# Register loads of the expert counts, with and without the sequencer's range check

## The chip, the cores and the metric

The kernel runs as one program on one core of a Trainium2 chip. The metric is the device time of one execution in microseconds (us), lower is better. The core has five engines that run beside each other and meet only at semaphores: TensorE (PE in the profile, its weight loads PEld), VectorE (DVE), ScalarE (ACT), GpSimd (POOL) and SyncE (SP, which issues most DMAs). Each engine takes its instructions strictly from its own queue. A small processor at the head of each queue, the sequencer (PEq, PEldq, SPq and so on in the profile), handles waits, register loads and register arithmetic itself.

## The reference

Causal attention with a data-dependent bias, then a dense layer pair with a gated activation, then a mixture of eight experts with one expert per token. The change touches the last part alone.

```python
logits = x @ w_gate                      # x: 1152 x 512, 8 experts
expert_idx = np.argmax(logits, axis=1)
...
for i in range(N):                       # each token takes the next place of its expert
    e = expert_idx[i]
    if counts[e] < capacity:
        disp[e, counts[e]] = x[i]
        counts[e] += 1
...
h = np.maximum(np.einsum('ecd,edf->ecf', disp, w1), 0.0)   # w1: 8 x 512 x 1024
y = np.einsum('ecf,efd->ecd', h, w2)                       # w2: 8 x 1024 x 512
out[i] = gate_w[i] * y[expert_idx[i], pos[i]]              # for the tokens that were kept
```

How many tokens an expert gets is known only on the chip.

## The kernel before

A planner (`pl.op`) takes every operation with its engine, what it reads and writes and a rank, and fixes at build time the order in which each engine's queue holds them. Nothing is reordered on the chip.

The expert stage starts near 334 us. The experts are sorted by their token counts, the fullest first, and run as experts e = 0 to 7 of this order with fixed tile widths WR = 224, 200, 184, 168, 152, 144, 136, 128. For each expert:

- `w_unit` loads the weights in 512 KB pieces through a ring of buffers (`wraw`, issued by SP at L1448 and L1450). ScalarE makes the rounded high part of each piece (L1455), VectorE the low part by a subtraction (L1456).
- `xs_in` loads the expert's rows (SP, L1518), TensorE transposes them (L1530), and ScalarE and VectorE split them again (L1534, L1536, L1539). A small VectorE copy (L1543) takes the gate and the token number out of the loaded rows.
- `e_mm1(e, fc)`, eight times: four matmuls with the high weights (L1568), which cover the high and the low activations side by side, so twice the tile width, and four with the low weights (L1572). ScalarE copies the right half out (L1582), VectorE adds (L1584), and L1586, L1588 and L1591 make the high, low and bf16 forms of the hidden values.
- `e_mm2(e, dc)`, four times: eight matmuls of each kind (L1605 high, L1607 low), then L1612 (ScalarE) and L1614 (VectorE) add the halves, and TensorE transposes the result back (L1619).
- the result is scaled by the gate and scattered to the output by a GpSimd DMA (L1641).

TensorE's queue interleaves `e_mm2` of expert e with `e_mm1` of expert e+1. Two PSUM banks serve `e_mm1` in turn (MI and MX in the profile).

The matmuls with low weights run over as many columns as the expert has tokens, not over the full width. The counts stand in `cntI` (8 integers in SBUF). The last two VectorE operations that make them cut them off above at the tile width and below at WMIN = 64. `widths()` brings them to TensorE: its sequencer loads the eight integers into registers (L1461) and sets eight shape registers from them, four at a time (L1463). The matmuls of experts 1 to 7 then take their width from these. Those of expert 0 have fixed widths. The planner puts `widths()` behind the last `e_mm1` of expert 0 and a group of transposes, and ahead of the first `e_mm2` of expert 0.

The profile names a buffer by the first tile that held its memory. So in the expert stage xT, gtH and their bf16 neighbours xTb, gtB hold activations and hidden values, wvi holds the sums of `e_mm1`, x2R rows, and x2Tt the result of `e_mm2`. AV, MI, MX and SC are PSUM banks.

Of the kernel before, what the change touches and what calls it, by code (L numbers as in the profile page):

```python
# [388 lines left out]
def fused_kernel(ctx, tc, q, k, v, s, w_in, w_out, w_gate, w1, w2, cap, out):  # L389
    nc = tc.nc  # L390
# [3 lines left out]
    E = w_gate.shape[1]  # L394
# [7 lines left out]
    W = 256  # L402
# [593 lines left out]
    with tc.manual_schedule():  # L996
# [89 lines left out]
        cntI = bp.tile([P, E], I32, name="cntI")  # L1086
        WMIN = 64
# [370 lines left out]

        def widths():
            def ld():  # L1460
                cs = nc.values_load_multi_w_load_instructions(cntI[0:1, 0:E], engines=[mybir.EngineType.PE], min_val=WMIN, max_val=W)[1]  # L1461
                for n in range(0, E, 4):
                    nc.tensor.move_shape(wreg[n:n + 4], [[(1, c)] for c in cs[n:n + 4]])  # L1463
            pl.op("pe", 600, ld, r=["cntI", ("hT", 0, 4)], w=["wreg"])
# [359 lines left out]
```

## Time and profile before

| | us |
|---|---|
| median of 3 runs | 491.97 |
| lowest and highest of them | 488.69, 493.15 |
| the profiled execution | 487.6 |
| its span, first to last instruction | 485.9 |
| busy in it: TensorE | 456.7 (94%) |
| busy in it: VectorE, ScalarE, GpSimd | 362.3, 332.5, 124.3 |

The rows come from the one profiled execution. Times in them are microseconds from the start of its span. Busy time doesn't count register loads, checks, branches or waits, which the sequencer handles. A bracket at the end of a row gives the idle time of the engine ahead of it and what ended it; "issue" means that no semaphore that the profile shows ended it. PEclk is the granted share of TensorE's 2.4 GHz clock (0.50 is 1.2 GHz).

### The profile page before, as it was taken

The numbers are of one execution on the slowest core, as the hardware profiler recorded it, in microseconds if no ns is written. First come the engines' busy times: TensorE is split into PE (matmuls) and PEld (weight loads), VectorE is DVE, ScalarE is ACT, GpSimd is POOL, SyncE is SP. The second block draws the span as 40 slices with busy tenths as digits, with TensorE's granted clock in tenths as the row PEclk, the third lists the DMA queues.
The fourth block names the chain that finished last, engine by engine and source line by source line (L and its number), as shares of the span: only waits on it lengthen the run. The fifth ranks groups of instructions, "written<-read, shape, count | busy, mean of one in ns | idle before, by whom it ended". The sixth has DMA issues, their size and how long they took to land.

```text
span 485.9 us, 9859 instructions
## 1 busy us (share of the span) xinstructions
PE 456.7 (94%) x3458; PEld 348.4 (72%) x3460; DVE 362.3 (75%) x826; ACT 332.5 (68%) x785; POOL 124.3 (26%) x136
## 2 busy tenths in 40 slices
PE   6698889999999999999999999999869999999993
PEld 5375566667777666668767867759768888889882
DVE  7889668988989999953123466937957979999891
ACT  3878879886657766744245246834958889989981
POOL 5627567477122222210000040002000201111141
PEclk9889989999999999999999999999989999999998
DMA  8999998699954554980000159841784867888811
GB/s 162 267 237 204 219 200 171 161 198 181 218 201 161 155 190 138 355 238 1 1 0 1 58 204 348 260 122 45 208 320 113 249 216 252 276 292 255 278 63 41
DMA packets 99049, 88.22 MB, mean 182 GB/s; under 512 B 66679, under 2 KB 77943, under 8 KB 98982
## 3 DMA queue, kind: packets, MB, share of 16 engines
q1 hardware_dynamic: 97108, 82.04, 62.4%
q0 software_dynamic: 1888, 5.52, 3.0%
q8 instruction: 28, 0.46, 0.4%
q14 instruction: 25, 0.20, 0.1%
HBM read 60.60 MB, written 14.19 MB: 154 GB/s over the span
## 4 chain that ended last, share of the span: by engine, by line
PE 72%; DMA 8%; ACT 8%; issue 4%; POOL 4%; DVE 2%; SPq 0%; POOLq 0%; ACTq 0%; DVEq 0%
PE SC L610 11%; PE MI L577 8%; PE MX L577 6%; PE AV L1605 6%; PE SC L611 5%; PE SC L863 4%; DMA PT<-ph 4%; PE MI L581 4%; PE MI L1568 3%; PE MX L1568 3%; PE AV L610 3%; PE MX L581 3%; POOL ph L908 2%; PE AV L941 2%; PE AV L1607 2%
## 5 line engine op out<-in xcount | busy, mean ns | idle before, releaser
L610 PE MATMUL SC<-woH,gtH 128*128 128x512 f32 x212 | 76.6, 479 | 0.0
L863 PE MATMUL SC<-QK 128*128 128x512 f32 (+4 forms) x192 | 63.0, 434 | 6.4 <-ACT pexp L894 3.4
L908 POOL TENSOR_TENSOR ph<-pexp,ph 128x512 f16<-128x512 f32 (+4 forms) x32 | 45.3, 1415 | 31.0 <-DVE ph L848 19.1
L591 DVE SCALAR_TENSOR_TENSOR gtH<-th,gtH 128x384 fp32r<-128x384 f32 x46 | 26.1, 569 | 32.8 <-ACT gtH L589 32.3
L577 PE MATMUL MI<-xT,wiH 128*128 128x384 f32 x216 | 47.1, 357 | 0.0
L894 ACT ACTIVATE pexp<-SC,smA 64x64 f32<-64x64 f32 (+4 forms) x80 | 38.3, 521 | 12.5 <-DVE smA L885 10.7
L594 ACT ACTIVATE gtB<-th 128x384 bf16<-128x384 f32 x46 | 23.8, 519 | 32.3 <-PE SC L611 26.1
L610 PEld LDWEIGHTS SC<-woH,gtH 128*128 128x128 f32 x212 | 40.0, 194 | 3.3
L863 PEld LDWEIGHTS SC<-QK 128*128 128x128 f32 (+1 forms) x192 | 28.3, 188 | 18.8 <-issue 11.2
L1456 DVE TENSOR_TENSOR wiL<-wraw,wiH 128x1024 bf16<-128x1024 f32 x32 | 38.8, 1219 | 3.5 <-ACT wiH L1455 3.5
L611 PE MATMUL SC<-woL,gtB 128*128 128x512 bf16 x106 | 41.4, 390 | 0.0
L1456 DVE TENSOR_TENSOR woL<-wraw,woH 128x1024 bf16<-128x1024 f32 x32 | 39.0, 1218 | 2.9 <-ACT woH L1455 2.8
L611 PEld LDWEIGHTS <-gtB 128*128 128x128 bf16 x138 | 13.3, 96 | 37.5 <-issue 37.5
L1271 POOL DMA_INDIRECT xs_d<-x2R,small x9 | 9.0, 998 | 121.0 <-ACT x2Tt L1204 69.0
L553 POOL TENSOR_TENSOR wiL<-wvi,wiH 128x512 bf16<-128x512 f32 x16 | 22.5, 1404 | 65.2 <-ACT wiH L549 65.2
L1641 POOL DMA_INDIRECT out_dram<-x2R,small x8 | 9.1, 1140 | 117.1 <-ACT x2R L1668 68.7
L577 PEld LDWEIGHTS MI<-xT,wiH 128*128 128x128 f32 x216 | 37.9, 189 | 1.3 <-DVE th L587 0.3
L577 PE MATMUL MX<-xT,wiH 128*128 128x384 f32 x168 | 36.7, 359 | 0.0
L1455 ACT ACTIVATE woH<-wraw 128x1024 fp32r<-128x1024 f32 x32 | 34.1, 1065 | 1.1 <-DMA wraw<-in_moe_w_dram 1.1
L1455 ACT ACTIVATE wiH<-wraw 128x1024 fp32r<-128x1024 f32 x32 | 33.6, 1055 | 1.6 <-DMA wraw<-in_moe_w_dram 1.6
L577 PEld LDWEIGHTS MX<-xT,wiH 128*128 128x128 f32 x168 | 30.0, 189 | 0.8
L941 PE MATMUL AV<-V,PT 128*128 128x65 f16 (+1 forms) x640 | 25.8, 197 | 4.6 <-DMA PT<-ph 4.6
(280 smaller groups left out, 1148.8 us busy)
## 6 DMA issues: line engine op xcount, KB each, us to landing
wraw<-in_moe_w_dram SPq DMA_DIRECT2D x64, 512.0 KB
wraw<-in_moe_w_in_dram SPq DMA_DIRECT2D x16, 512.0 KB
wraw<-in_moe_w_out_dram SPq DMA_DIRECT2D x16, 512.0 KB
xs_d<-x2R SPq DMA_DIRECT2D x16, 257.0 KB
kraw<-in_k_dram SPq DMA_DIRECT2D x8, 288.0 KB
qraw<-in_q_dram SPq DMA_DIRECT2D x8, 288.0 KB
out_dram<-x2R SPq DMA_DIRECT2D x9, 256.0 KB
x2R<-xs_d SPq DMA_DIRECT2D x8, 257.0 KB
```

The source lines that it names most:

```text
L577: nc.tensor.matmul(ps, lhsT=whi[:, kc], rhs=xT[:, a, kc, cs], start=(kc == 0 and a == 0), stop=False)
L581: nc.tensor.matmul(ps, lhsT=wlo[:, kc], rhs=xTb[:, kc, cs], start=False, stop=(kc == KC - 1))
L610: nc.tensor.matmul(o, lhsT=gh[:, a, ts], rhs=whi, start=(fc == 0 and a == 0), stop=False)
L611: nc.tensor.matmul(o, lhsT=gb[:, ts], rhs=wlo, start=False, stop=(fc == NFC - 1))
L863: nc.tensor.matmul(o[:rows, j0:j1], lhsT=t_[:, 2 * r, i0:i0 + rows], rhs=t_[:, 2 * r + 1, j0:j1], start=True, stop=False)
L894: pl.op("act", t_act(wdt, False, 1), lambda o=o, r=r, nm=nm: nc.scalar.activation(out=pe[:rows, r, :wdt], in_=o[:rows, :wdt], func=AF.Exp, ...
L908: pl.op(eng, (t_pool if eng == "pool" else t_dve)(n * T_), lambda rs_=rs_, e_=e_: e_.tensor_tensor(out=hl[:, rs_, 0:T_], in0=pe[:rows, rs_ ...
L941: nc.tensor.matmul(av[:, slot, r, 0:D + 1 - h_], lhsT=PT[t][:, r * (1 + 2 * t) + pb, :], rhs=rhs, start=(i == 0), stop=(i == len(m) - 1))
L1455: pl.op("act", t_act(1024), lambda: nc.scalar.activation(out=dhi, in_=raw, func=AF.Copy), r=[rk], w=kh, rank=rank, after=after)
L1456: pl.op("dve", t_dve(1024), lambda: nc.vector.tensor_tensor(out=dlo, in0=raw, in1=dhi.bitcast(F32), op=ALU.subtract), r=[rk, ks[0], ks[2]] ...
L1568: nc.tensor.matmul(ps[:, 0:2 * w_], lhsT=uH[s_][kc][:, fs], rhs=xs[:, kc], start=(kc == 0), stop=False)
L1605: nc.tensor.matmul(ps[:, 0:2 * w_], lhsT=uH[s_][KC + fc // 2][:, ds_[fc]], rhs=h[:, fc], start=(fc == 0), stop=False)
```

## The change

The register load is told not to check the values' range on the chip. The minimum and maximum stay as what the build may assume of the values.

```diff
         def widths():
             def ld():
-                cs = nc.values_load_multi_w_load_instructions(cntI[0:1, 0:E], engines=[mybir.EngineType.PE], min_val=WMIN, max_val=W)[1]
+                cs = nc.values_load_multi_w_load_instructions(cntI[0:1, 0:E], engines=[mybir.EngineType.PE], min_val=WMIN, max_val=W,
+                                                                   skip_runtime_bounds_check_because="the counts are bounded on VectorE")[1]
                 for n in range(0, E, 4):
                     nc.tensor.move_shape(wreg[n:n + 4], [[(1, c)] for c in cs[n:n + 4]])
```

The added source line moves every later line number up by one. On TensorE's queue, behind the transposes of an expert's rows (SC from x2R) and ahead of the first `e_mm2` of expert 0 (AV), there stood the load of the counts, sixteen sequencer instructions, which are eight pairs of a register operation and an assertion, and the two settings of four shape registers each.

```order
L1530 MATMUL SC_105<-identF,x2R 128x128 x2
L1530 MATMUL SC_105<-identF,x2R 128x72 x2
L1461 TENSOR_LOAD cntI
L1461 ISA x16
L1463 ISA x2
L1605 MATMUL AV_107<-xT,wiH_1939 128x448 x2
```

Now the same place on the same queue has the load and the two settings alone.

```order
L1531 MATMUL SC_105<-identF,x2R 128x128 x2
L1531 MATMUL SC_105<-identF,x2R 128x72 x2
L1461 TENSOR_LOAD cntI
L1464 ISA x2
L1606 MATMUL AV_107<-xT,wiH_1939 128x448 x2
```

The sixteen are gone. No other instruction of this queue and none of the other four has moved, and no wait is added or taken away.

## Rows read from the trace of the kernel before

**Rows 1.** Lines 1461 and 1463: count, ns shortest/median/longest, first and last start.

```profile
L1461 PEldq FUSED_REGOPS  x8: 146/146/160, 353.6 to 355.7; - x8
L1461 PEldq SEQ_ASSERT  x8: 18/18/28, 353.8 to 355.9; - x8
...
L1461 PEldq TENSOR_LOAD <-cntI x1: 780/780/780, 352.7 to 352.7; - x1
...
L1463 PEldq MOVE  x2: 29/31/33, 355.9 to 356.2; - x2
L1463 PEld MOVE_SHAPE  x2: 113/116/118, 356.0 to 356.3; - x2
```

**Rows 2.** TensorE timeline, 351 to 358 us: start, us, engine.

```profile
352.23 0.52 PE L1530 MATMUL SC<-identF,x2R 128*128 128x128 f32 x4
356.46 1.83 PE L1605 MATMUL AV<-xT,wiH 128*128 128x448 f32 x4 [3.72 <-issue]
```

**Rows 3.** Windows of 1 us, with their column names.

```profile
core 0: us, PE busy (x) PEld busy (x) DVE busy (x) ACT busy (x) POOL busy (x), PEclk, DMA share, GB/s
...
355.00:356.00 1.00, 0.00 (x0) 0.00 (x0) 0.00 (x0) 0.41 (x2) 0.00 (x0) 0.94 1.03 320
...
359.00:360.00 1.00, 1.00 (x9) 0.72 (x8) 0.19 (x1) 0.00 (x0) 0.00 (x0) 0.86 0.86 311
```

**Rows 4.** Chain that ended last, from 356 us: start, us, what.

```profile
356.46 3.15 PE AV L1605 x8
...
360.40 0.74 PE MI L1568 x4
...
362.48 0.22 PE SC L1619 x2
362.70 0.74 PE MI L1568 x4
...
365.25 1.81 PE AV L1605 x8
367.06 0.78 PE AV L1607 x8
```

**Rows 5.** ScalarE and VectorE timeline around the wait: start, us, engine.

```profile
353.47 0.29 DVE L1588 SCALAR_TENSOR_TENSOR xT<-wvi,xT 128x128 fp32r<-128x128 f32 x1
...
356.62 0.16 DVE L1543 COPY small<-x2R 56x2 f32<-56x2 f32 x1 [1.91 <-DMA x2R<-xs_d]
...
357.98 1.21 DVE L1456 TENSOR_TENSOR wiL<-wraw,wiH 128x1024 bf16<-128x1024 f32 x1
360.83 0.39 DVE L1614 TENSOR_TENSOR x2Tt<-AV,x2R 128x224 f32<-128x224 f32 x1 [1.64 <-ACT x2R L1612]
361.89 0.37 DVE L1584 TENSOR_TENSOR wvi<-MI,wvi 128x200 f32<-128x200 f32 x1 [0.67 <-ACT wvi L1582]
```

**Rows 6.** TensorE timeline, 352 us to the end: its later waits.

```profile
434.32 0.44 PE L1530 MATMUL SC<-identF,x2R 128*128 128x128 f32 x2 [0.46 <-ACT gtB L1539]
...
460.97 0.44 PE L1619 MATMUL SC<-identF,x2Tt 128*128 128x128 f32 x2 [0.48 <-DVE x2Tt L1614]
```

**Rows 7.** Timeline of ScalarE, 368 to 436 us.

```profile
377.75 0.36 ACT L1612 ACTIVATE x2R<-AV 128x224 f32<-128x224 f32 x1 [1.11 <-PE AV L1607]
...
414.46 0.30 ACT L1582 ACTIVATE wvi<-MI 128x152 f32<-128x152 f32 x1 [0.38 <-PE MI L1572]
```

**Rows 8.** Timeline of all engines, 470 us to the end.

```profile
478.20 0.69 ACT L1653 ACTIVATE x2R<-SC,small 128x512 f32<-128x512 f32 x1 [1.64 <-PE SC L1634]
```

**Rows 9.** Timeline of TensorE, 60 to 70 us.

```profile
66.09 1.71 PE L941 MATMUL AV<-V,PT 128*128 128x65 f16 x28 [1.36 <-DMA PT<-ph]
```

**Rows 10.** Windows around earlier waits of TensorE, columns as above.

```profile
66.10:69.10 3.00, 3.00 (x35) 2.83 (x36) 1.24 (x4) 0.94 (x4) 0.30 (x1) 0.50 1.29 188
...
105.40:106.60 1.20, 0.11 (x5) 0.08 (x3) 0.47 (x2) 1.15 (x4) 0.22 (x1) 1.00 1.05 234
...
21.40:28.10 6.70, 5.11 (x43) 4.19 (x44) 5.63 (x7) 4.33 (x10) 3.08 (x2) 0.50 1.21 198
```

## The prediction

> **What bounds the kernel now.** I first looked for where the removed instructions ran, in the source view of their line [rows 1]. The load of the counts takes 0.78 us from 352.7. Behind it come eight pairs, a FUSED_REGOPS of 146 ns and a SEQ_ASSERT of 18 ns, from 353.6 on; the first setting of shape registers begins only at 355.9. Next I read what TensorE did meanwhile [rows 2]: its transposes end at 352.75 (352.23 plus 0.52), the next matmul starts at 356.46, and the 3.72 us between are put down to "issue", that is, to no semaphore. So the wait is the sequencer's own work, and the reader sees in it the load, the checks and the settings, end to end.
>
> Third, the granted clock [rows 3]. It fell to half within the window from 355, whose mean is 0.94: a share of (1 - 0.94)/0.5 = 0.12 us at half speed, so it fell at 355.88, after TensorE had done nothing for 3.1 us. The window from 359 gives 0.86, so 0.28 us at half speed, and the clock rose at 359.28, after 2.8 us of dense matmuls. The two `e_mm2` groups of equal shape show the price [rows 4]: the first takes 360.40 - 356.46 = 3.94 us, the second 1.81 + 0.78 = 2.59. The wait therefore cost a further 1.35 us behind itself.
>
> Fourth, is TensorE the bound behind 356? Its timeline shows only two waits of it on another engine from there to the end, 0.46 us at 434.32 and 0.48 at 460.97 [rows 6]. ScalarE on its side waited for TensorE, 1.11 us at 377.75 and still 0.38 us at 414.46 [rows 7], and its last scaling at 478.20 waited for TensorE's last matmul [rows 8]. A lead won at 356 should thus travel to the end, unless something beside TensorE holds the start of the stage.
>
> **The change part by part.** *The checks.* Sixteen instructions go, and nothing takes their place. Their price is the time from the first of them to the first setting, 355.9 - 353.6 = 2.3 us, or 0.29 us a pair; the pairs' own 164 ns would give 1.3 us, but the gaps between sequencer instructions go with them. Nothing covers them, since TensorE's queue is in order and idle. The load's 0.78 us and the settings' 0.5 us stay. The first `e_mm2` then starts at 356.46 - 2.3 = 354.16. Its inputs are there: the last hidden value of expert 0 is made at 353.47 + 0.29 = 353.76 [rows 5]. If the register values were late behind the load, the settings would wait; the row before shows the first check 0.1 us behind the load's end, so I put this at 0 to 0.1 us and take 0.
>
> *The clock.* TensorE's idle time shrinks to 3.72 - 2.3 = 1.4 us. I look for waits of that length [rows 9, 10]. One of 1.09 us, in the window from 105.4, kept the full clock (1.00, with 0.11 us busy out of 1.2). One of 1.36 us ahead of 66.09, in a stretch of 64-column matmuls, was followed by half speed (0.50 from 66.1 to 69.1). Here matmuls of 256 columns stand ahead of the wait and of 448 behind it, which is far denser work than at 66, so I take it that the clock stays; the other case is a rival.
>
> The Trainium skill, page "TensorE: Matmul & The Clock Gate", section "HAM oscillation — how this bites in real kernels", prices time at the half clock at half its length. For 355.88 to 359.28 this is an estimate of 1.7 us against 1.35 by the rows, where TensorE still stood idle for the first 0.58 us of it. The removed wait would be worth 4.0 us by the page and 3.65 by the rows; the next step cuts either to the same sum.
>
> *What is late next.* With the full clock the first `e_mm2` ends at 354.16 + 2.59 = 356.75. The two `e_mm1` groups of expert 1 behind it took 362.48 - 360.40 = 2.08 us [rows 4], so TensorE reaches the transposes L1619 at 358.83. These need VectorE's sum L1614, and here the rows of VectorE decide [rows 5]. Its copy L1543 waited 1.91 us for a DMA and began at 356.62; two weight subtractions stand behind it, the second from 357.98 to 359.19, and only then L1614. (ScalarE's copy L1612, which L1614 also needs, is no later: L1614 began 0.43 us behind the matmuls' end at 360.40, which would be 357.2.) In the old trace VectorE then idled 1.64 us for TensorE. Now TensorE waits for it: nothing of this VectorE work depends on TensorE's wait, so it stays where it is. L1614 runs from 359.19 to 359.58, L1584 (0.37 us) to 359.95. The third `e_mm1` of expert 1 needs that addition, because it writes the bank that L1584 empties. It starts at 359.96 instead of 362.70, 2.7 us earlier. So of 3.65 us won at the first matmul 0.9 is given back within 5 us.
>
> *Behind it.* VectorE's own queue moves by 361.89 - 359.58 = 2.3 us, and ScalarE, the conversions and the loads that they release follow it. TensorE had 0.4 us to spare on that addition (ended 362.26, used at 362.70), so 2.3 to 2.7 us reach the dense stretch; I take 2.7, because ScalarE's idle 1.11 us at 377.75 absorbs the difference. No instruction elsewhere changes, and the tail behind 478 keeps its length.
>
> The sum: -2.3 (checks) - 1.35 (clock) + 0.9 (VectorE) = -2.7 us. The profiled execution would go from 487.6 to 484.9. The median shown is 491.97, 4.4 above that execution, and I carry the difference over: 489.3 us, 0.5% less. About 1% is what a measurement of this kernel can tell from no change; its three runs alone lie 0.9% apart.
>
> **The rivals.** *The clock falls all the same.* For it speaks the wait of 1.36 us at 66, against it the one of 1.09 at 105 and the denser work here. Taking one stretch as long as 355.88 to 359.28 (3.4 us), TensorE loses 1.7 us, the point 358.83 becomes 360.53, VectorE no longer holds anything, and the third `e_mm1` starts near 360.75: 2.0 us won, 490.0 us. The Trainium skill, page "TensorE: Matmul & The Clock Gate", section "What's actually happening", calls the throttled state the default that activity lifts; by it two short waits could bring the fall that one long one brought here.
>
> *The lead is lost at 434.* There TensorE waited 0.46 us for ScalarE [rows 6], behind weight conversions. If those ran at the pace of their loads and not of TensorE, TensorE would come 2.7 us earlier and wait 2.7 us longer, and 0 to 0.5 us would remain: 491.5 to 492.0. Against it: ScalarE waited for TensorE at 414.46 [rows 7], so its run up to 434 was released by TensorE and moves with it.
>
> *VectorE doesn't hold.* If the load behind its copy at 356.62 lands earlier in most executions, all 3.65 us stay: 488.3.
>
> *The checks cost nothing of their own*, because the registers' arrival sets the pace: then the settings start no earlier, and the time stays 492.0. Against it, the pairs run in equal steps to the end with no long first one.
>
> *Slower.* The clock falls at the first short wait and, since a second wait of 0.8 us follows at 358.8, isn't given back for long. At 21.4 to 28.1 it stayed at half for 6.7 us although TensorE was busy for 5.1 of them [rows 10]. A stretch of that length costs about 3.4 us of matmul time against the 3.65 won, so it is no loss yet. From a little over 7 us on the kernel is slower; three stretches like the 3.4 us one (10.2 us) would cost 5.1 and give 493.4. Against it, the dense matmuls behind the wait lifted the clock within 2.8 us in this very place.
>
> **How the numbers follow.** Forecast 489.3: 0.60. Clock falls all the same, 490.0: 0.15. Lead lost at 434, 491.5 to 492.0: 0.12. VectorE doesn't hold, 488.3: 0.06. Checks cost nothing, 492.0: 0.04. Slower, 493.4: 0.03. A median of three runs that spread over 4.5 us moves by an estimated third of that, 1.5. The range goes from 488.3 less 1.8 to 490.0 plus 1.9, so 486.5 to 491.9, and leaves out about the three upper rivals. A gain of over 1% (below 487.05) needs the forecast or the 488.3 and a lucky scatter of two or three us: 0.13. A loss of over 1% needs more than the slower rival's 493.4: 0.02. The rest, 0.85, lies within 1%.
>
> **What would show it.** In the profile after: no FUSED_REGOPS or SEQ_ASSERT on line 1461, the first setting some 0.1 us behind the load, and TensorE idle 1.4 us there instead of 3.72. PEclk 1.00 from 350 to 365, the first `e_mm2` in 2.6 us. A new wait of TensorE on VectorE's L1614 of 0.7 to 0.9 us near 359, VectorE's own rows up to 359.2 unmoved, the third `e_mm1` of expert 1 near 360.0. Waits of 0.5 us near 431 and 458, the last matmul 2.7 us earlier. I would be wrong if the settings still start near 355.9, if PEclk shows 0.50 behind the wait, or if a wait at the two late places has grown by the lead.

## The result and the profile after

The changed kernel takes 485.37 us (median of 20 runs, 483.65 to 489.75). The kernel before, on the same chip, takes 490.96 (20 runs, 487.97 to 495.03). The ratio is 0.990, 95% interval 0.9876 to 0.9925, so 4.9 us less, with an interval of 3.7 to 6.1. The prediction had 489.3 us and 2.7 us less; the lower end of its range was 486.5. The profiled execution took 485.11, with a span of 483.4.

The source view of the two lines after, against [rows 1]: count, ns shortest/median/longest, first and last start.

```profile
L1461 PEldq TENSOR_LOAD <-cntI x1: 780/780/780, 353.0 to 353.0; - x1
L1464 PEldq MOVE  x2: 29/31/33, 353.9 to 354.2; - x2
L1464 PEld MOVE_SHAPE  x2: 113/115/117, 354.0 to 354.3; - x2
```

The sixteen checks are gone, the load is as long as it was, and the first setting comes 0.1 us behind its end. TensorE's timeline after, with every row from 353 us to the end that shows a wait, against [rows 2, 6]:

```profile
352.50 0.52 PE L1531 MATMUL SC<-identF,x2R 128*128 128x128 f32 x4
354.44 1.86 PE L1606 MATMUL AV<-xT,wiH 128*128 128x448 f32 x8 [1.43 <-ACT xT L1535]
...
359.80 0.44 PE L1620 MATMUL SC<-identF,x2Tt 128*128 128x128 f32 x2 [0.64 <-DVE x2Tt L1615]
360.07 1.00 PE L1569 MATMUL MI<-xT,woH 128*128 128x400 f32 x4
...
432.43 0.44 PE L1531 MATMUL SC<-identF,x2R 128*128 128x128 f32 x2 [1.07 <-ACT gtB L1540]
```

The transposes end at 353.02, and the wait behind them is 1.43 us instead of 3.72. The row names ScalarE's L1535, which ended at 354.29. But the second setting ends at 354.4, and the weight load of the first matmul starts at 354.41, right behind it; so the settings end the wait. The first eight matmuls take 1.86 us; before, they took 3.15 [rows 4]. A wait on VectorE's L1615 is new, at 359.8. The third `e_mm1` of expert 1, which starts at 360.07 here, started at 362.46 before:

```profile
362.46 0.98 PE L1568 MATMUL MI<-xT,woH 128*128 128x400 f32 x4
```

Windows of the same stretch, against [rows 3]:

```profile
core 0: us, PE busy (x) PEld busy (x) DVE busy (x) ACT busy (x) POOL busy (x), PEclk, DMA share, GB/s
353.00:354.00 1.00, 0.01 (x1) 0.00 (x0) 0.89 (x5) 1.00 (x6) 0.00 (x0) 1.00 0.86 328
354.00:355.00 1.00, 0.56 (x3) 0.79 (x6) 0.92 (x5) 1.00 (x2) 0.00 (x0) 1.00 0.83 267
355.00:356.00 1.00, 1.00 (x7) 0.86 (x5) 0.00 (x0) 0.63 (x2) 0.00 (x0) 1.00 1.01 375
356.00:358.00 2.00, 2.00 (x19) 1.69 (x18) 1.12 (x3) 1.30 (x2) 0.00 (x0) 1.00 1.00 316
358.00:360.00 2.00, 1.36 (x12) 0.98 (x10) 2.00 (x7) 0.34 (x1) 0.00 (x0) 1.00 1.02 359
```

PEclk stays at 1.00 (2.4 GHz). VectorE's timeline after, against [rows 5]:

```profile
356.88 0.16 DVE L1544 COPY small<-x2R 56x2 f32<-56x2 f32 x1 [1.90 <-DMA x2R<-xs_d]
...
357.02 1.21 DVE L1456 TENSOR_TENSOR wiL<-wraw,wiH 128x1024 bf16<-128x1024 f32 x1
...
358.24 1.21 DVE L1456 TENSOR_TENSOR wiL<-wraw,wiH 128x1024 bf16<-128x1024 f32 x1
359.37 0.37 DVE L1615 TENSOR_TENSOR x2Tt<-AV,x2R 128x224 f32<-128x224 f32 x1
359.67 0.34 DVE L1585 TENSOR_TENSOR wvi<-MI,wvi 128x200 f32<-128x200 f32 x1
```

The copy waits for the row load as long as before, the two subtractions follow it without a gap, and L1615 no longer waits for TensorE: TensorE waits for it. The lead then lasts to the end. ScalarE's last scaling, against [rows 8]:

```profile
475.71 0.69 ACT L1654 ACTIVATE x2R<-SC,small 128x512 f32<-128x512 f32 x1 [1.64 <-PE SC L1635]
```

TensorE's last matmul, before and after:

```profile
477.77 0.39 PE L1634 MATMUL SC<-woL,xTb 128*128 128x512 bf16 x1
```

```profile
475.28 0.39 PE L1635 MATMUL SC<-woL,xTb 128*128 128x512 bf16 x1
```

From the end of the transposes to the end of the last matmul it is 475.67 - 353.02 = 122.65 us; before it was 478.16 - 352.75 = 125.41. In these two executions the place gives 2.8 us, and the tail behind the last matmul is 7.73 in both. So the local steps came nearly as forecast, and yet the times differ by more. That is what the experiments are about.

### The profile page after: what moved, and what is told of

Its sections match the earlier page's. It is cut to its first block, busy times and chain, and to the rows that moved or that the text cites. A ratio compares the mean times of both kernels' runs of the same rounds, so it can differ in the third digit from the quotient of the medians.

```text
span 483.4 us, 9843 instructions
## 1 busy us (share of the span) xinstructions
PE 458.7 (95%) x3458; PEld 349.3 (72%) x3460; DVE 362.7 (75%) x826; ACT 332.4 (69%) x785; POOL 122.9 (25%) x136
## 4 chain that ended last, share of the span: by engine, by line
PE 73%; ACT 8%; DMA 7%; issue 4%; DVE 4%; POOL 2%; POOLq 0%; SPq 0%; ACTq 0%; DVEq 0%
PE SC L610 11%; PE MI L577 8%; PE MX L577 6%; PE AV L1606 6%; PE SC L611 5%; PE SC L863 5%; DMA PT<-ph 4%; PE MI L581 4%; PE MI L1569 3%; PE AV L610 3%; PE MX L581 3%; PE MX L1569 3%; PE AV L941 3%; PE AV L1608 2%; ACT pexp L894 2%
## 5 line engine op out<-in xcount | busy, mean ns | idle before, releaser
L863 PE MATMUL SC<-QK 128*128 128x512 f32 (+4 forms) x192 | 64.7, 444 | 3.4 <-ACT pexp L894 3.4
L1456 DVE TENSOR_TENSOR wiL<-wraw,wiH 128x1024 bf16<-128x1024 f32 x32 | 38.8, 1218 | 3.5 <-ACT wiH L1455 3.5
L1456 DVE TENSOR_TENSOR woL<-wraw,woH 128x1024 bf16<-128x1024 f32 x32 | 38.9, 1217 | 3.1 <-ACT woH L1455 3.1
L1455 ACT ACTIVATE wiH<-wraw 128x1024 fp32r<-128x1024 f32 x32 | 33.6, 1055 | 2.0 <-DMA wraw<-in_moe_w_dram 2.0
L1455 ACT ACTIVATE woH<-wraw 128x1024 fp32r<-128x1024 f32 x32 | 34.0, 1063 | 0.5 <-DMA wraw<-in_moe_w_dram 0.5
```

The costliest lines, as they stand in the source:

```text
L863: nc.tensor.matmul(o[:rows, j0:j1], lhsT=t_[:, 2 * r, i0:i0 + rows], rhs=t_[:, 2 * r + 1, j0:j1], start=True, stop=False)
L1455: pl.op("act", t_act(1024), lambda: nc.scalar.activation(out=dhi, in_=raw, func=AF.Copy), r=[rk], w=kh, rank=rank, after=after)
L1456: pl.op("dve", t_dve(1024), lambda: nc.vector.tensor_tensor(out=dlo, in0=raw, in1=dhi.bitcast(F32), op=ALU.subtract), r=[rk, ks[0], ks[2]] ...
```

## The experiments

Three theories stood against each other. *The place with a larger clock term*: all of the gain arises between the transposes and the third `e_mm1` of expert 1, and the one execution read beforehand had a small clock loss. *The place as forecast*: 2.7 us, and the rest of the measured gain is scatter. *Somewhere else*: fewer entries in TensorE's queue help beyond the place. In the expectations the first is theory A, and the last is B (the difference lies in the attention part) or D (the shorter queue shifts something ahead of the place). The rival C of shapes8 is that the assertion itself costs.

All eighteen traces are read with one table. The edits of copyb and apad are described further down. Columns: "first", from the end of the transposes to the first `e_mm2` of expert 0; "middle", from there to the third `e_mm1` of expert 1; "half", time at half clock in between; "last", from the end of the transposes to the end of the last matmul. Each is a difference of starts and ends in TensorE's timeline (of the kernel after: 354.44 - 353.02, 360.07 - 354.44).

```
                          first  middle  half   last
checks kept
  before                   3.72    5.99   3.4  125.4
  b2                       3.73    6.12   3.4  125.0
  b3                       3.72    6.23   3.4  126.0
  b4                       3.71    7.15   6.8  126.7
  copyb                    3.72    7.22   6.8  127.0
  b1                       3.70    7.44   6.8  126.4
  mean of the six          3.72    6.69        126.1
checks gone
  a3                       1.41    4.68   0    121.4
  apad                     1.37    5.33   0    122.5
  after                    1.43    5.63   0    122.7
  a2                       1.41    5.79   0    122.4
  a1                       1.41    6.42   0    124.6
  mean of the five         1.41    5.57        122.7
other edits
  copylate                 1.43    4.69   0    121.5
  shapes8                  3.52    4.68   0    123.3
  fill                     4.12    4.70   0    124.4
  half                     2.60    6.29   3.4  123.8
  late                    -0.20    5.68   0    121.4
  late2                   -0.20    6.63   0    121.8
  bothlate                -0.20    6.09   0    121.1
```

**b1, b2, b3, b4: the kernel before, unchanged.**

These four have no edit.

> The kernel before, unchanged, for more executions and a second trace of it. Theory A (the place): the typical execution loses more in this very place than the profiled one did, by the clock. Then the time is 490 to 492, and in the trace the stretch from the end of the transposes ahead of the load to TensorE's last matmul takes 125.4 us as in the first trace or up to 3 more, with half clock behind the wait. Theory B (elsewhere): the stretch takes 125.4 us within 0.3 in every execution, and what differs between executions lies ahead of 352 us, in the attention stage.

> The kernel before, unchanged, for a third trace. Theory A: the third first-layer group stands 8.3 (no fall), 9.7 (a fall of 3.4 us) or 11.1 us (6.8 us) behind the transposes' end. Theory B: 9.7 again, and the time follows the attention stage.

> The kernel before, unchanged, for a fourth trace, with the same two expectations.

> The kernel before, unchanged, for a fifth trace and as a measure of what two builds of one kernel differ by: 0.998 to 1.002. From the transposes' end to the last matmul 125 to 126.4 us.

b1 came to a ratio of 0.9979 (0.9954 to 1.0005), b4 to 1.0006 (0.9979 to 1.0034), so identical kernels compare as equal within a quarter of a per cent. b2 and b3 are single executions of 495.59 and 491.59 us. b4's stretch of 126.7 us lies 0.3 above what was expected of it. What these traces add is the clock. TensorE's timeline and the windows of b1:

```profile
357.31 3.32 PE L1605 MATMUL AV<-xT,wiH 128*128 128x448 f32 x8 [3.70 <-issue]
```

```profile
356.00:357.00 1.00, 0.00 (x0) 0.12 (x1) 0.00 (x0) 0.23 (x1) 0.00 (x0) 0.69 1.01 361
...
360.00:362.00 2.00, 2.00 (x11) 1.33 (x11) 0.59 (x1) 0.00 (x0) 0.00 (x0) 0.50 0.98 349
362.00:363.00 1.00, 1.00 (x5) 0.97 (x4) 0.39 (x1) 0.36 (x1) 0.00 (x0) 0.50 1.05 387
363.00:364.00 1.00, 1.00 (x9) 0.73 (x8) 0.00 (x0) 0.19 (x1) 0.00 (x0) 0.90 1.00 338
```

The wait is the same 3.7 us, but the clock is back only at 363.2, behind six us of dense matmuls, where the profile shown beforehand had it back after 2.8. Three of the six traces with the checks show a half clock of 3.4 us, three one of 6.8. b2 also shows where the scatter of the times is made, far ahead of the change. A row of its TensorE timeline:

```profile
81.32 1.71 PE L941 MATMUL AV<-V,PT 128*128 128x65 f16 x28 [2.08 <-DMA PT<-ph]
```

Behind such waits in the attention part the clock fell more or less often, 10.2 to 20.4 us of half clock in these traces, and the transposes ended anywhere from 352.75 (before) to 361.09 (b2). With the checks gone the same point lies at 353.0 to 357.2, and the ranges overlap. The stretch behind the transposes differs by no more than 2.0 us between the six (125.0 to 127.0), and the tail behind it by no more than 0.1; so the larger part of the 4.4 us between the profiled execution of before and the median must come from ahead of the place, if the executions without a trace are like these.

**a1, a2, a3: the changed kernel, unchanged.**

These three have no edit.

> The kernel after, unchanged, for a second trace. Theory A: 485 to 486, the stretch from the transposes to the last matmul 122.4 to 122.9 us (122.65 in the first trace), full clock behind the wait. Theory B: the same stretch, and a time that follows the part ahead of 352 us.

> The kernel after, unchanged, once more. Theory A (only this place, 2.1 to 3.0 us by the traces so far): 0.994 of before, and the rest of the measured gain is scatter of the attention stage. Theory D (the shorter queue also shifts something ahead of the place): 0.990 again, and in the trace the transposes ahead of the load end earlier than in before, near 353 us.

> The changed kernel unchanged, as the row that the other three are compared with, and a sixth trace of it (the fourth of the plain form). If only the place between the transposes and the third first-layer group of expert 1 gives the gain, as the traces so far say (2.7 to 2.9 us), the ratio is 0.994 and the pooled times come down to it. If the times so far are right (4.2 us), it is 0.9915. In the trace the third group should start 3.2 us behind the start of VectorE's small copy out of the loaded rows, whenever that begins, and the clock should show no fall there.

The ratios are 0.9915 (0.9883 to 0.9947), 0.9935 (0.9900 to 0.9969) and 0.9935 (0.9902 to 0.9968). With the first comparison the mean of four is 0.9921, or 3.9 us of 490.5; as four independent comparisons they leave it uncertain by 0.8 us either way. In a2 the transposes end at 357.2, not near 353 as theory D had it. The clock fell in none of these traces. The copy L1544 starts at 356.88 in the first trace after, 361.30 in a1 and 361.19 in a2, and the third `e_mm1` 3.2 us behind it each time (360.07, 364.49, 364.39). In a3 it came early. VectorE's and TensorE's rows of a3:

```profile
357.56 0.16 DVE L1544 COPY small<-x2R 56x2 f32<-56x2 f32 x1 [0.74 <-DMA x2R<-xs_d]
```

```profile
356.25 1.85 PE L1606 MATMUL AV<-xT,wiH 128*128 128x448 f32 x8 [1.41 <-ACT xT L1535]
...
360.80 0.38 PE L1620 MATMUL SC<-identF,x2Tt 128*128 128x128 f32 x2
360.94 0.97 PE L1569 MATMUL MI<-xT,woH 128*128 128x400 f32 x4
```

The copy starts 2.7 us behind the transposes (354.85) instead of 3.5 to 4.6, L1620 no longer waits, and the middle shrinks to 4.68. The late copy is also a part of why a1's stretch was 124.6 us, where 122.4 to 122.9 were expected: its middle is 0.8 us longer than that of the first trace after. The other 1.1 us lie behind the third `e_mm1`.

Not only the traces speak of the clock. Every run has its mean granted clock on record, over the whole span. In a1, a2 and a3 it is 0.985, 0.984 and 0.984 on average, in the runs of the kernel before beside them 0.978, 0.979 and 0.980. As time at half clock, twice the missing share of the span, that is 6.8, 5.0 and 3.5 us less, 5.1 on average. The six traces with the checks had 3.4 or 6.8 us in the place, 5.1 on average, and the five without had none. The measure doesn't say where in the span the clock fell, but its amount fits, so the falls in these six traces look typical. It is rough: b1 and b4, which are the kernel before itself, differ by about 2 us from the runs of before beside them.

**shapes8: the checks' time without the checks.** The settings are made five times.

```diff
-                for n in range(0, E, 4):
+                for n in 5 * list(range(0, E, 4)):
                     nc.tensor.move_shape(wreg[n:n + 4], [[(1, c)] for c in cs[n:n + 4]])
```

> Without checks, but the eight counts are written into the shape registers five times instead of once: eight more settings of 0.27 us, 2.15 us of the sequencer's time in the place where the checks stood, and sixteen queue entries as they had. Theory A (only the time in this place counts): first matmul of the first second-layer group near 356.3, clock falls, 490 to 491.5, the gain all but gone. Rival C (the assertion itself costs, by more than its time in the queue): 485 to 487.

The ratio is 1.0003 (0.9975 to 1.0030): the gain is gone. It is the time on TensorE's queue in this place that costs, not what fills it. In the profiled execution (485.82, the fastest of its 12) the clock did not fall. Its row and window:

```profile
356.58 1.86 PE L1606 MATMUL AV<-xT,wiH 128*128 128x448 f32 x8 [3.52 <-ACT xTb L1540]
```

```profile
356.00:357.00 1.00, 0.42 (x2) 0.66 (x5) 1.00 (x2) 0.62 (x1) 0.00 (x0) 1.00 1.05 398
```

So a wait of 3.5 us is not always followed by the half clock. Without the fall the middle is 4.68. But this execution is not typical of the twelve: their mean clock is 0.978, that of the kernel before beside them, and this one has 0.990, the next highest 0.980. So in the others the clock most likely fell as it did with the checks.

**half: four of the eight counts checked.** The edit is against the kernel before.

```diff
-                cs = nc.values_load_multi_w_load_instructions(cntI[0:1, 0:E], engines=[mybir.EngineType.PE], min_val=WMIN, max_val=W)[1]
+                cs = nc.values_load_multi_w_load_instructions(cntI[0:1, 0:E], engines=[mybir.EngineType.PE])[1]
+                why = "the counts are bounded on VectorE"
+                cs = [nc.s_assert_within(c, WMIN, W, skip_runtime_bounds_check_because=None if n < 4 else why) for n, c in enumerate(cs)]
```

> Four of the eight counts are checked. The wait of TensorE should be 1.43 + 1.15 = 2.6 us. If TensorE's arrival set the time alone, half the gain, 488. By the prediction's chain VectorE releases the third first-layer group of expert 1 at 360, so TensorE may come 0.9 us late at no cost: with the clock kept, the wait costs 1.15 - 0.65 = 0.5 us, 486; with the clock fallen 1.2 to 1.7 us more, 487 to 488.

The ratio is 0.9972 (0.9942 to 1.0003). TensorE's wait is cut by half as well, and the clock still falls:

```profile
355.47 2.11 PE L1607 MATMUL AV<-xT,wiH 128*128 128x448 f32 x8 [2.60 <-ACT wiH L1455]
```

```profile
356.00:358.00 2.00, 2.00 (x11) 1.42 (x10) 1.46 (x5) 1.06 (x1) 0.00 (x0) 0.73 0.94 352
```

The fall began at 356.92, when TensorE had been at work again for 1.45 us. 2.60 us is the mean of 3.72 and 1.42 within 0.03, so a pair costs 0.28 to 0.30 us, with four as with eight. With half the checks the place is 1.5 us shorter than the mean with all of them (2.60 + 6.29 against 10.41); the ratio stands for 1.4.

**fill: the checks kept, TensorE kept busy under them.** Sixteen matmuls into an idle bank run ahead of the load; they add nothing to the result.

```diff
             def ld():
+                for _ in range(16):
+                    nc.tensor.matmul(BK[3], lhsT=uH[0][KC][:, 0:P], rhs=uH[0][KC][:, 0:512], start=True, stop=True)
                 cs = nc.values_load_multi_w_load_instructions(cntI[0:1, 0:E], engines=[mybir.EngineType.PE], min_val=WMIN, max_val=W)[1]
```

> The kernel before with all its checks, and sixteen matmuls of 512 columns ahead of the load, into a PSUM bank that the second group of the second layer clears anyway. They run while the sequencer loads and checks. They add nothing to the result. Theory A (checks plus a clock fall whose price differs between executions): the sequencer's path stays, first real matmul 3.7 us behind the transposes, but the clock can't fall; third first-layer group of expert 1 about 8.3 us behind the transposes' end (9.7 and 11.1 in the two traces of before), 487 to 488. Theory B (the price lies elsewhere): 490 as before.

```profile
356.20 3.92 PE L1462 MATMUL AV<-wiH 128*128 128x512 f32 x16
360.52 1.87 PE L1607 MATMUL AV<-xT,wiH 128*128 128x448 f32 x8 [0.40 <-issue]
```

```profile
360.00:362.00 2.00, 1.60 (x8) 1.65 (x10) 1.23 (x1) 0.00 (x0) 0.00 (x0) 1.00 0.83 286
```

The clock stayed at 1.00, and the middle is 4.70, that of shapes8, against 5.99 to 7.44. The load began later behind the matmuls, so the first `e_mm2` is 0.4 us later. The net gain by the table is 10.41 - 8.82 = 1.6 us; the ratio, 0.9986 (0.9961 to 1.0011), stands for 0.7, and its interval reaches from 1.9 less to 0.5 more. So the expected 487 to 488 us was missed: the median of 490.33 is nearer to theory B's 490. For theory A speaks the clock, in the trace and in the twelve runs (a mean of 0.985 against 0.981 before, 3.9 us less at half clock); what that is worth in time, these times can't tell from nothing.

**apad: sixteen queue entries put back where nothing waits for them.** Eight settings are made behind TensorE's last matmul.

```diff
+        held_cs = []
...
+                held_cs.extend(cs)
...
+        for n in 4 * list(range(0, E, 4)):
+            nc.tensor.move_shape(wreg[n:n + 4], [[(1, c)] for c in held_cs[n:n + 4]])
```

> The kernel after with the sixteen queue entries put back at the far end of TensorE's queue, as eight more settings of the shape registers behind its last matmul, where nothing waits for them. Theory A: as after, 0.990 to 0.994. Theory D, if it is the length of the queue: as before, 0.998 to 1.000.

The ratio is 0.9946 (0.9915 to 0.9977). The source view of the added line, and the place:

```profile
L1719 PEldq MOVE  x8: 29/29/29, 474.5 to 476.3; - x8
L1719 PEld MOVE_SHAPE  x8: 112/113/113, 474.6 to 476.4; - x8
```

They are not free: the tail behind the last matmul is 8.98 us instead of 7.73. Less these 1.25 us the time is 486.4, that of the changed kernel, and the place measures as there (1.37 and 5.33). So the number of entries shows no effect of its own, and the theory of a gain elsewhere has no support.

**late, late2: the load moved to where TensorE's queue has work.** The load and the settings stand behind the first `e_mm2` of expert 0.

```diff
-            pl.op("pe", 600, ld, r=["cntI", ("hT", 0, 4)], w=["wreg"])
+            pl.op("pe", 600, lambda: None, r=["cntI", ("hT", 0, 4)], w=["wreg"])
+            return ld
...
+                if e == dc == 0:
+                    set_widths[0]()
...
-                widths()
+                set_widths.append(widths())
```

> The kernel after, with the unchecked load moved behind the first second-layer group of expert 0, so that its sequencer time hides behind sixteen matmuls. No other instruction moves. By the prediction's chain VectorE holds the third first-layer group at the same moment, 7.1 us behind the transposes' end, and TensorE just waits for it 1.4 us longer: 485 to 486, no change from after. If TensorE's own arrival were the bound, 484.

> The load behind the first second-layer group once more, beside after on one chip. In its first trace the stretch from the transposes ahead of the first second-layer group to the last matmul took 121.4 us against 122.7 and 124.6 of after. If that holds, 1 to 2 us below after; if VectorE holds the third first-layer group as the prediction had it, the same as after.

```profile
355.51 1.86 PE L1607 MATMUL AV<-xT,wiH 128*128 128x448 f32 x8
...
358.90 0.97 PE L1570 MATMUL MI<-xT,woH 128*128 128x400 f32 x4 [0.75 <-issue]
```

The first `e_mm2` no longer waits at all, and half of the load's wait is found again ahead of the next group. The third `e_mm1` comes 0.5 to 1.5 us nearer to the transposes than the mean of the five, but the ratios, 0.9934 (0.9904 to 0.9964) and 0.9939 (0.9907 to 0.9971), are those of a2 and a3.

**copylate: VectorE's copy put behind the sums.** The copy of expert 2's second tile, which waits for a row load, stands 23 places later in VectorE's queue; nothing else moves.

```diff
-                      r=[("x2r", i, 0)], w=[("meta", e % 4, j)])
+                      r=[("x2r", i, 0)] + ([("hTl", 1, 1)] if e == 2 and j == 1 else []), w=[("meta", e % 4, j)])
```

> The changed kernel, with VectorE's small copy of expert 2 that waits for a row load put 23 places later in its queue. Theory VectorE's copy caps the gain: the two weight subtractions then start when ScalarE has made their high parts (355.3 and 357.3 us in the first trace after), VectorE's sum of the first second-layer group starts near 358.6, and the third first-layer group of expert 1 near 359.4 instead of 360.07, 0.7 us earlier, less where the row load lands later: up to 1.5. Time 0.7 to 1 us under that of a3, ratio about 0.990. Rival, the weight loads set the pace: the second subtraction stays where it is, and place and time equal a3's.

VectorE's timeline, then all rows of TensorE from 353 us on that show a wait:

```profile
354.39 1.23 DVE L1456 TENSOR_TENSOR wiL<-wraw,wiH 128x1024 bf16<-128x1024 f32 x1
...
355.73 1.23 DVE L1456 TENSOR_TENSOR wiL<-wraw,wiH 128x1024 bf16<-128x1024 f32 x1
356.87 0.38 DVE L1615 TENSOR_TENSOR x2Tt<-AV,x2R 128x224 f32<-128x224 f32 x1
```

```profile
353.56 1.86 PE L1606 MATMUL AV<-xT,wiH 128*128 128x448 f32 x8 [1.43 <-ACT xT L1535]
430.54 0.44 PE L1531 MATMUL SC<-identF,x2R 128*128 128x128 f32 x2 [1.05 <-ACT gtB L1540]
```

Without the copy's wait L1615 is done well ahead of TensorE, and TensorE's wait on it is gone. The middle is 4.69, the value of a3, shapes8 and fill, where VectorE does not hold either. So the copy is the cap where its row load comes late, as the 3.2 us between it and the third `e_mm1` in four of the five traces say. (When that load landed in copylate's own execution, its trace doesn't show.) The cap takes 5.57 - 4.69 = 0.9 us on average. The ratio is 0.9918 (0.9879 to 0.9957) against a3's 0.9935 in the same comparison: not told apart, since the cap is not there in every execution of a3 either (its trace shows none), and 0.9 us is below what 12 runs resolve.

**copyb: the same move with the checks kept.**

```diff
-                      r=[("x2r", i, 0)], w=[("meta", e % 4, j)])
+                      r=[("x2r", i, 0)] + ([("hTl", 1, 1)] if e == 2 and j == 1 else []), w=[("meta", e % 4, j)])
```

> The kernel before, checks kept, with the same move of the copy. Both theories: in it VectorE waited for TensorE behind the copy (1.64 us), so nothing is late by it, the third group stays 9.7 to 11 us behind the transposes, ratio 1.000. If it comes out at 0.997 or less, the copy's wait costs time elsewhere too, and copylate's result says nothing of the cap.

The ratio is 1.0034 (1.0000 to 1.0069): no gain, perhaps a loss. TensorE's first `e_mm2` and VectorE's L1614:

```profile
359.66 3.32 PE L1605 MATMUL AV<-xT,wiH 128*128 128x448 f32 x8 [3.72 <-issue]
```

```profile
364.93 0.39 DVE L1614 TENSOR_TENSOR x2Tt<-AV,x2R 128x224 f32<-128x224 f32 x1 [3.55 <-ACT x2R L1612]
```

VectorE is early by 3.55 us and gains nothing by it. It was early without the move too, by 1.64 in the trace of before and 4.03 in b4. As long as TensorE waits for the checks, the copy costs nothing.

**bothlate: both moves.**

```diff
-            pl.op("pe", 600, ld, r=["cntI", ("hT", 0, 4)], w=["wreg"])
+            pl.op("pe", 600, lambda: None, r=["cntI", ("hT", 0, 4)], w=["wreg"])
+            return ld
...
-                      r=[("x2r", i, 0)], w=[("meta", e % 4, j)])
+                      r=[("x2r", i, 0)] + ([("hTl", 1, 1)] if e == 2 and j == 1 else []), w=[("meta", e % 4, j)])
...
+                if e == dc == 0:
+                    set_widths[0]()
...
```

> The changed kernel with the copy moved and the load of the counts moved behind the first second-layer group of expert 0. If VectorE's copy was what kept the move of the load from paying, this is the fastest of all: the first group starts 1.6 us earlier, TensorE alone would reach the third group near 357.8, but ScalarE's weight part at 356.2 to 357.3 and VectorE behind it hold it at 359.4. So by the cap through ScalarE's part and its weight load it equals copylate, ratio about 0.990; by TensorE alone it is 1.6 us below it, 0.987.

ScalarE's, VectorE's and TensorE's rows:

```profile
359.09 1.06 ACT L1455 ACTIVATE wiH<-wraw 128x1024 fp32r<-128x1024 f32 x1 [0.33 <-DMA wraw<-in_moe_w_dram]
```

```profile
360.18 1.23 DVE L1456 TENSOR_TENSOR wiL<-wraw,wiH 128x1024 bf16<-128x1024 f32 x1 [0.47 <-ACT wiH L1455]
361.32 0.38 DVE L1618 TENSOR_TENSOR x2Tt<-AV,x2R 128x224 f32<-128x224 f32 x1
```

```profile
359.31 0.96 PE L1570 MATMUL MI<-xT,woH 128*128 128x400 f32 x4 [0.71 <-issue]
...
361.76 0.44 PE L1623 MATMUL SC<-identF,x2Tt 128*128 128x128 f32 x2
```

With the copy out of the way the chain is weight load, L1455, L1456, L1618, TensorE: ScalarE waits 0.33 us for a load, VectorE 0.47 for ScalarE, and the sum is made just ahead of the transposes. The third `e_mm1` comes 5.9 us behind the transposes, against copylate's 6.1. The ratio is 0.9930 (0.9891 to 0.9969): the 0.987 by TensorE alone lies outside, the 0.990 by the cap inside. None of late, copylate and bothlate is told apart from the changed kernel, so no version is offered that beats it.

## Why the prediction was right, and where it was wrong

*The checks, -2.3 us: right.* "First" went from 3.72 to 1.41 us, five times out of five. That the price was the time from first check to first setting, not the pairs' own 164 ns, is borne out by half.

*The clock stays behind a wait of 1.4 us: right.* No fall in any of the five traces, so neither the rival of the clock that falls all the same nor the slower one, built on it, came about.

*The clock's price, -1.35 us: the term that failed.* The prediction said "The wait therefore cost a further 1.35 us behind itself", from the one execution it had. With the clock kept and VectorE not holding, the middle is 4.68 to 4.70 (a3, shapes8, fill, copylate). The three traces of before's order with one fall of 3.4 us have 6.11 on average, a loss of 1.4: the reading was right for its execution. The other three, with 6.8 us, have 7.27, a loss of 2.6. The mean of the six is 6.69 - 4.69 = 2.0 us. The rivals asked whether the clock would fall in the kernel after; none asked whether the fall in the kernel before was a typical one, although the prediction's own rows held one of 6.7 us elsewhere [rows 10].

The Trainium skill, page "TensorE: Matmul & The Clock Gate", section "HAM oscillation — how this bites in real kernels", takes half of the throttled time as its price, which gives an estimate of 1.7 us for 3.4 and 3.4 for 6.8. The traces give 1.4 and 2.6. TensorE stood idle for the first part of the fall, 0.6 us in before and 0.9 in b1; half of the rest is 1.4 and 2.9, against 1.3 and 2.75 measured. The measurement decides.

*VectorE takes back +0.9: right.* The mean of the five is 0.9 (5.57 against 4.69), from nothing in a3 to 1.7 in a1, as the row load lands. The rival "VectorE doesn't hold" is thus not an alternative but a part of the executions, one of five here.

*The lead reaches the end: right.* From the third `e_mm1` to the last matmul it is 115.7 us on average in the five and in the six. In the first trace after TensorE waits 1.07 us at 432, where about 0.5 was forecast, and the second late wait, at 461, is gone.

*One reading was off.* The 2.7 us are counted from 362.70 [rows 4], where the chain lets the third `e_mm1` begin only when the piece before it ends. In TensorE's timeline it starts at 362.46, so the working gives 2.5 us, and TensorE had 0.2 to spare on the addition, not 0.4. The first pair of traces has 9.71 - 7.05 = 2.7.

*The sum.* -2.3 - 2.0 + 0.9 = -3.4 us is what the table gives, by the mean of "first" and "middle" (10.41 to 6.98), and by "last" (126.1 to 122.7). The four comparisons give 3.9 on average, uncertain by 0.8: the table's 3.4 lies inside, the forecast's 2.7 outside. The first comparison alone, 3.7 to 6.1, lies just above the table's 3.4. The table is no sharper, since "last" goes from 121.4 to 124.6 among the five. No trace shows a further source, and nothing here excludes a small one.

*The forecast time.* It lay 3.9 us above the measured median. Of these 0.7 are the clock term. Another 1.0 is the start: the median of three, 491.97, stood above that of twenty, 490.96. The other 2.2 us are the first comparison itself, whose 5.6 us between medians the three repeats did not reach (3.2 to 4.2 by their ratios). No trace accounts for these 2.2, and their cause stays open; they may be scatter. The range took in the scatter of a median and the named rivals, but no other size of the clock's loss. With 2.0 in place of 1.35 its lower end would have been near 485.9, still above the 485.37 measured, so the clock term alone doesn't make up the miss.

## What to carry to other kernels

A loss that follows from a state of the chip, like the clock's half speed behind a wait, has a spread of its own: read it in several executions before it becomes one number in a sum. Before forecasting what a removed wait is worth, run the queue of the engine that was early (here VectorE) forward without it: its rows gave the cap within 0.2 us of the first trace after, 7.2 behind the transposes against 7.06; the other four lay between 6.1 and 7.8. Put a forecast on the ratio, not on a median of three runs that spread over four us.

## What the hardware showed that was not expected

- The same wait of 3.7 us on the same instructions was followed by a half clock (1.2 GHz) of 3.4 us in three executions and 6.8 in three. In one execution with 3.52 us (shapes8) there was none; in one with 2.60 (half) there was one of 3.4, which began 1.45 us after TensorE was back at work.
- A register operation and an assertion on TensorE's queue cost 0.28 to 0.30 us a pair, though their own durations are 146 and 18 ns.
- Eight settings of four shape registers at the very end of TensorE's queue made the tail 1.25 us longer in the one trace of it, although they need no other engine and overlap the last matmuls in part.
- A stage that ends 352.75 us into one execution ends at 361.09 in another of the same kernel, with 10.2 and 20.4 us of half clock ahead of it.
